# Scan pattern and reciprocals moved to SBUF, one forward scan for four pairs of heads, filler products alone in a PSUM bank, early low halves on VectorE

## The chip, the core and the metric

The kernel runs on one core of a Trainium2 chip. Its time is the device time of one execution in microseconds (us); the median of three runs is compared. The engines are TensorE (PE; its weight loads are listed as PEld), VectorE (DVE), ScalarE (ACT), GpSimd (POOL) and SyncE (SP), which issues most of the transfers. Each engine takes its instructions in the order in which the program lists them.

## The reference

A linear attention with a decay per channel feeds a mixture of experts with two choices a token, and that feeds a dense block (batch 4, 8 heads, 768 steps, head size 48; 3072 tokens of 384; 8 experts of 1024; dense width 2048).

```python
for t in range(S):                                   # attention
    state = alpha[:, :, t, :, None] * state + np.einsum('bhd,bhe->bhde', k[:, :, t], v[:, :, t])
    y[:, :, t] = np.einsum('bhd,bhde->bhe', q[:, :, t], state)
...
noisy_logits = x @ w_gate + np.log1p(np.exp(x @ w_noise)) * noise      # experts
top2 = np.argpartition(-noisy_logits, 2, axis=1)[:, :2]
...
    h = np.maximum(x[mask] @ w1[e], 0.0)
    out[mask] += top2_w[mask, k, None] * (h @ w2[e])
...
h = x @ w_in                                         # dense block
g = np.maximum(0.01 * h, h)
return (g @ w_out).astype(np.float32)
```

## The kernel before

The attention is cut into 24 units of 128 steps (`build_unit`), six for each batch row, in order. A unit holds four pairs of heads; its tables are 112 rows high, one pair side by side, so an operation over a unit is 112 x 512 (four pairs of 128 steps). `at` holds the decays, `kq` the keys and queries, `nv` the values; each is loaded once a unit by SyncE. For a unit VectorE does this:

- `back` (L965): a scan over all 512 columns from the right, `suf`, the product of the decays behind each step. Its second operand is a byte pattern that starts each pair anew.
- `forth` (L973, L974), twice, for two pairs each: the reciprocals of the pairs' totals are put into the first column of each pair of a float pattern, and a scan over 256 columns from the left with that pattern as its second operand gives `wt`.
- `keys` (L988) and `queries` (L992): `kt = k * suf` and `qp = q * wt`.

Both patterns lie in one PSUM tile, `pC`, of 512 columns: 256 for the float pattern of two pairs, 128 for the byte pattern, and the last 128 are where filler products are written (`warm`). Filler products (L919, `keep_busy`) are products of the identity with itself whose result nobody reads; they keep TensorE at work where the planner sees a pause.

From `kt` and `qp` TensorE makes the turned keys (`pM`, L1000), the scores (`pS`, L1013), the state's update (L1048, L1052), and the outputs within and across units (`pY`, L1069, L1076), and turns the output back with the router's logits beside it (`pA`, L1098). ScalarE copies the results out (`kN`, `ar`, `S`, `xt`, `xg`). GpSimd masks the scores (`am`, L1022, two a unit), multiplies the state by the decays' totals (`sp`, L1039) and makes the totals (`tots`, L978). After each four units (a tile) the router runs (`gate_top2` and what follows, all small operations `g_...`, `run`, `sel`, `pk`, `si`), and GpSimd scatters the four blocks of tokens to their experts' slots (L1191, two for each block).

The weights of an expert come in pieces of 384 KB; each is split into a high half by ScalarE (L464) and a low half, the rest, by `split_lo` (L468): `w1lA`, `w2lA` for expert 0 and `w1lB`, `w2lB` for half the pieces behind it. The low halves stand as "vg": VectorE or GpSimd, whichever the planner has free. The expert stage begins with the first product of L742 once the rows of the first group are turned (`xl`, L609) and the last tile's counts are through TensorE (L1162, L538).

The order of all engines is made by `Planner`, which plays the steps through with an estimated duration for each, a due time, and rings that say how many buffers of a tile there are. Where it sees TensorE pause for longer than `GAP`, it puts filler products in front of the next step, as many as the pause divided by `FILL` (or, for the first, by `COLD`).

Of the kernel before, what the change touches and what calls it, by code (L numbers as in the profile page):

```python
# [7 lines left out]
FT = mybir.dt.float32  # L8
# [3 lines left out]
U32 = mybir.dt.uint32  # L12
AF = mybir.ActivationFunctionType
OP = mybir.AluOpType
# [5 lines left out]
PERIOD = 6.0  # L20
# [13 lines left out]
TYD = 8.0  # L34
# [35 lines left out]
class Planner:  # L70

    NEAR, FAR, SLACK, RATE, LAND = 0.1, 0.25, 0.8, 0.26, 2.0
    GAP, FILL, COLD, AHEAD, MARGIN = 0.45, 0.24, 0.45, 0.3, 3.0

# [261 lines left out]
def tile_kernel(  # L336
# [21 lines left out]
    nc = tc.nc  # L358
# [5 lines left out]
    NG, C = 4, 128  # L364
    P2, HP, NC = 2 * D, H // 2, S // C

    PP = 64 + D
# [98 lines left out]
    def split_lo(i, which, en):  # L466
        hi, lo = WT[i][2 * which:2 * which + 2]
        (nc.vector if en == "v" else nc.gpsimd).tensor_sub(lo, RAW[i, which], hi.bitcast(FT))  # L468
# [180 lines left out]
    def build_experts(t0, R, scat, last_x, ready_at, totals, acc_done, begun):  # L649
# [33 lines left out]
        def expert_weights(i, after):  # L683
            e = PAIRS[i][1]
            prev = [WO[i - 1]] if i else []
            phase = 1 if e == 0 else 2
            AUX[i] = []
            for m, nm in enumerate(("w1s", "w2s")):
                fe = add("s", 0.45, lambda m=m: fetch(i, m), after, takes=[R[nm]], size=0.39)
                hi = add("a", 0.73, lambda m=m: split_hi(i, m), prev, use=[(fe, R[nm])] + ([(WO[i], R["W"])] if m else []),  # L690
                         takes=[] if m else [R["W"]], phase=phase)
                if m == 0:
                    WO[i] = hi
                AUX[i].append([hi, add("vg", dict(v=0.87, g=1.8), lambda en, m=m: split_lo(i, m, en), [hi],
                                       use=[(fe, R[nm]), (WO[i], R["W"])], phase=phase)])
# [208 lines left out]
    with ExitStack() as actx:  # L904
# [3 lines left out]
        psum = actx.enter_context(tc.tile_pool(name="psum", bufs=1, space=PSUM))  # L908
        bank = psum.tile([128, 512], FT, name="pC", bufs=1)
        scb, warm = bank[:PP, 0:HB * C + C], bank[:, HB * C + C:]  # L910
        nc.vector.memset(scb, 0.0)
        d1f = scb[:, 0:HB * C].rearrange("p (h c) -> p h c", c=C)
        d1b = scb[:, HB * C:].bitcast(mybir.dt.uint8)

        nc.vector.memset(scb[:, HB * C:].bitcast(U32).rearrange("p (h c) -> p h c", c=C // 4)[:, :, C // 4 - 1:], 1 << 24)

# [15 lines left out]
        def build_unit(u):  # L932
            d = st[u]
            b = at_unit(u)
            hc = HB * C
            prev = st[u - 1] if u else None
# [31 lines left out]

            def forth(i):
                if i == 0:  # L970
                    d["wt"] = work.tile([PP, NW], FT, name="wt", bufs=3)
                    d["wv"] = d["wt"].rearrange("p (h c) -> p h c", c=C)
                nc.vector.reciprocal(d1f[:, :, 0], d["sv"][:, i * HB:(i + 1) * HB, 0])  # L973
                nc.vector.tensor_tensor_scan(d["wt"][:, i * hc:(i + 1) * hc], d["at"][:, i * hc:(i + 1) * hc],  # L974
                                             scb[:, 0:hc], 0.0, OP.mult, OP.add)

# [5 lines left out]
            totals.append(tt)  # L982
            f0 = add("v", 0.8, lambda: forth(0), [b1], use=[(LA, R["at"]), (b0, R["suf"])], takes=[R["wt"]])
            f1 = add("v", 0.8, lambda: forth(1), [f0], use=[(LA, R["at"]), (b0, R["suf"]), (f0, R["wt"])])

# [124 lines left out]
            cy = add("a", 0.5, copy_y, [done], use=[(w0, R["pY"])], takes=[R["xt"]])  # L1110
            ty = add("p", 0.8, turn_y, [consts_in], use=[(cy, R["xt"])], takes=[R["pA"]], due=b + PERIOD + TYD)
            cx = add("a", 0.39, copy_x, use=[(ty, R["pA"])], takes=[R["xg"]])
# [369 lines left out]
```

## Time and profile before

| What | us |
|---|---|
| median of three runs | 1079.25 (1076.63 to 1081.55) |
| the profiled execution, its own time | 1087.71 |
| its span | 1085.9 |
| TensorE busy in the span | 1042.8 (96%) |
| VectorE busy | 593.7 (55%) |
| ScalarE busy | 388.2 (36%) |
| GpSimd busy | 278.5 (26%) |

The shares are means over two stages that have little in common: the attention with the router, up to 178.6 us, and the expert and dense products after it. Times in the rows are us from the span's start. A row of the timeline has a start, a duration, engine, line, operation, `out<-in`, shapes, and in brackets the idle time of the engine ahead of it and what ended it. TensorE does a product of 32-bit floats in two passes, so 11 products of the program are 22 rows of the trace.

### The profile page before, as it was taken

What the parts mean: (1) busy time and instruction counts of PE and PEld (TensorE: products, weight loads), DVE (VectorE), ACT (ScalarE), POOL (GpSimd) and SP (SyncE); (2) the same over time, 40 slices, a digit from 0 to 9 for tenths busy, and PEclk for the clock granted to TensorE, in tenths of its full rate; (3) what the DMA queues carried; (4) which work ended last, traced back from release to release, by engine and by line L of the source; (5) the groups of instructions that cost most, each with busy time, mean ns of one, the idle gap of its engine ahead of it and who ended that gap; (6) DMA issues with size and microseconds to landing.
All of it is one profiled execution on the core that took longest, in us unless ns stands there. A gap on an engine that the chain in (4) does not pass through costs nothing.

```text
span 1085.9 us, 18172 instructions
## 1 busy us (share of the span) xinstructions
PE 1042.8 (96%) x6839; PEld 999.2 (92%) x6839; DVE 593.7 (55%) x1218; ACT 388.2 (36%) x825; POOL 278.5 (26%) x321
## 2 busy tenths in 40 slices
PE   6999895999999999999999999999999999999997
PEld 5887775999999999999999989899999999999997
DVE  5998997223464565646574233455554545454543
ACT  3755644223354544445453222222222222212211
POOL 3466876200032253424351021410110100000000
PEclk9998997999999999999999999999999999999999
DMA  9667746413464565746567344320101100000000
GB/s 232 203 203 242 237 129 222 157 50 103 148 201 141 179 200 164 226 142 207 180 222 241 116 153 139 92 66 9 59 22 45 34 33 16 22 1 23 1 22 26
DMA packets 78917, 133.20 MB, mean 123 GB/s; under 512 B 8514, under 2 KB 56260, under 8 KB 78820
## 3 DMA queue, kind: packets, MB, share of 16 engines
q1 hardware_dynamic: 72292, 111.89, 33.2%
q0 software_dynamic: 6528, 20.06, 5.7%
q8 instruction: 56, 0.92, 0.4%
q14 instruction: 41, 0.34, 0.1%
HBM read 93.38 MB, written 38.54 MB: 121 GB/s over the span
## 4 chain that ended last, share of the span: by engine, by line
PE 87%; DVE 8%; issue 2%; DMA 1%; ACT 1%; another core or an unknown queue 1%; POOL 0%; DVEq 0%; ACTq 0%; POOLq 0%
PE py L781 39%; PE ph L742 39%; PE pA L600 2%; DVE wt L974 1%; PE pS L1013 1%; DVE suf L965 1%; PE pA L1098 1%; PE pY L1069 1%; PE pC L919 1%; PE pY L1076 1%; DVE kt L988 1%; PE pM L1048 1%; DMA xg<-y_d,gidx 1%; DVE g_z L225 0%
## 5 line engine op out<-in xcount | busy, mean ns | idle before, releaser
L766 DVE SCALAR_TENSOR_TENSOR hl<-ph,hh 128x384 fp32r<-128x384 f32 (+1 forms) x128 | 77.4, 606 | 192.3 <-ACT hh L759 186.1
L752 ACT ACTIVATE hc<-ph 128x384 f32<-128x384 f32 x128 | 63.0, 492 | 300.6 <-PE ph L742 283.3
L755 DVE SCALAR_TENSOR_TENSOR hc<-hc 128x384 f32<-128x384 f32 x128 | 71.4, 558 | 178.2 <-ACT hc L752 178.2
L759 ACT ACTIVATE hh<-ph 128x384 fp32r<-128x384 f32 (+1 forms) x128 | 68.0, 532 | 241.7 <-PE ph L742 236.0
L781 PE MATMUL py<-w2hA,hh 128*128 128x384 f32 (+1 forms) x416 | 141.5, 340 | 1.1 <-issue 1.1
L781 PE MATMUL py<-w2hB,hh 128*128 128x384 f32 (+1 forms) x416 | 141.9, 341 | 0.2 <-issue 0.2
L781 PE MATMUL py<-w2lB,hh 128*128 128x384 f32 (+1 forms) x416 | 140.5, 338 | 0.4 <-issue 0.4
L781 PE MATMUL py<-w2hB,hl 128*128 128x384 f32 (+1 forms) x416 | 140.5, 338 | 0.0
L781 PE MATMUL py<-w2hA,hl 128*128 128x384 f32 (+1 forms) x416 | 140.0, 337 | 0.0
L781 PE MATMUL py<-w2lA,hh 128*128 128x384 f32 (+1 forms) x416 | 139.9, 336 | 0.0
L742 PE MATMUL ph<-xh,w1hA 128*128 128x384 f32 (+1 forms) x384 | 136.4, 355 | 1.4 <-ACT hc L752 0.7
L742 PE MATMUL ph<-xl,w1hA 128*128 128x384 f32 (+1 forms) x384 | 134.3, 350 | 1.0 <-issue 1.0
L742 PE MATMUL ph<-xh,w1hB 128*128 128x384 f32 (+1 forms) x384 | 134.1, 349 | 0.4 <-DVE hl L766 0.4
L742 PE MATMUL ph<-xh,w1lA 128*128 128x384 f32 (+1 forms) x384 | 134.1, 349 | 0.0
L742 PE MATMUL ph<-xl,w1hB 128*128 128x384 f32 (+1 forms) x384 | 133.4, 347 | 0.0
L742 PE MATMUL ph<-xh,w1lB 128*128 128x384 f32 (+1 forms) x384 | 133.3, 347 | 0.0
L804 POOL DMA_INDIRECT xg<-y_d,gidx x48 | 46.5, 968 | 279.6 <-PE pA L600 172.7
L781 PEld LDWEIGHTS py<-w2lA,hh 128*128 128x128 f32 (+1 forms) x416 | 77.3, 186 | 2.2 <-issue 1.2
L781 PEld LDWEIGHTS py<-w2lB,hh 128*128 128x128 f32 (+1 forms) x416 | 77.6, 187 | 1.3 <-issue 0.3
L781 PEld LDWEIGHTS py<-w2hB,hh 128*128 128x128 f32 (+1 forms) x416 | 77.5, 186 | 0.8
L769 DVE TENSOR_TENSOR hl<-hc,hh 128x384 fp32r<-128x384 f32 x128 | 71.4, 558 | 12.3 <-DVE hh L761 0.5
L781 PEld LDWEIGHTS py<-w2hB,hl 128*128 128x128 f32 (+1 forms) x416 | 77.6, 187 | 0.5 <-issue 0.5
(160 smaller groups left out, 1877.3 us busy)
## 6 DMA issues: line engine op xcount, KB each, us to landing
w1s<-in_moe_w_dram SPq DMA_DIRECT2D x32, 384.0 KB
w2s<-in_moe_w_dram SPq DMA_DIRECT2D x32, 384.0 KB
kq<-in_kq_l_dram SPq DMA_DIRECT2D x24, 448.0 KB
nv<-in_v_l_dram SPq DMA_DIRECT2D x24, 256.0 KB
w1s<-in_moe_w_in_dram SPq DMA_DIRECT2D x24, 256.0 KB
w2s<-in_moe_w_out_dram SPq DMA_DIRECT2D x16, 384.0 KB
xg<-x_s SPq DMA_DIRECT2D x32, 180.0 KB
y_d<-ys SPq DMA_DIRECT2D x32, 180.0 KB
```

The costliest lines, as they stand in the source:

```text
L600: nc.tensor.transpose(p[:, d, :n], src[:n, d * 128:(d + 1) * 128], identf[:n, :n])
L742: nc.tensor.matmul(ps[:, :n], a[:, d, fo:fo + 128], x[:, d, :n], start=i == 0, stop=i == len(seq) - 1)
L752: nc.scalar.activation(hc[:, :n], ps[:, :n], AF.Copy)
L755: nc.vector.scalar_tensor_tensor(hc[:, :n], hc[:, :n], 0.01, hc[:, :n], op0=OP.mult, op1=OP.max)
L759: nc.scalar.activation(hh[:, :n], ps[:, :n], AF.Relu)
L766: nc.vector.scalar_tensor_tensor(hl[:, :n], ps[:, :n], 0.0, hh[:, :n].bitcast(FT), op0=OP.max, op1=OP.subtract)
L769: nc.vector.tensor_sub(hl[:, :n], HT[si, "hc"][:, :n], hh[:, :n].bitcast(FT))
L781: nc.tensor.matmul(py[:n, :], h[:, o:o + n], w[:, f % 2, :], start=(f == 0 and i == 0), stop=(f == nf - 1 and i == 2))
L804: nc.gpsimd.indirect_dma_start(out=yg, out_offset=None, in_=y_d[0:rows, :], in_offset=bass.IndirectOffsetOnAxis(ap=gidx[:, c, kk:kk + 1], ...
L919: nc.tensor.matmul(warm, identf, identf, start=True, stop=True)
L965: nc.vector.tensor_tensor_scan(rev(d["suf"][:, :]), rev(d["at"][:, 1:NW + 1]), rev(d1b), 0.0, OP.mult, OP.add)
L974: nc.vector.tensor_tensor_scan(d["wt"][:, i * hc:(i + 1) * hc], d["at"][:, i * hc:(i + 1) * hc], scb[:, 0:hc], 0.0, OP.mult, OP.add)
```

## The change

The byte pattern and the float pattern become tiles of their own in SBUF, the float pattern now for four pairs; `forth` is one reciprocal of four columns and one scan of 512. The filler products keep `pC` for themselves, a tile of 128 columns. The low halves of expert 0 may go on VectorE alone. Four numbers of the planner change: two prices of a filler product, the price of the turn (`ty`), and the forward scan's.

```diff
-    GAP, FILL, COLD, AHEAD, MARGIN = 0.45, 0.24, 0.45, 0.3, 3.0
+    GAP, FILL, COLD, AHEAD, MARGIN = 0.45, 0.16, 0.22, 0.3, 3.0
...
-                AUX[i].append([hi, add("vg", dict(v=0.87, g=1.8), lambda en, m=m: split_lo(i, m, en), [hi],
+                AUX[i].append([hi, add("vg" if phase == 2 else "v", dict(v=0.87, g=1.8) if phase == 2 else 0.87, lambda en="v", m=m: split_lo(i, m, en), [hi],
...
-        bank = psum.tile([128, 512], FT, name="pC", bufs=1)
-        scb, warm = bank[:PP, 0:HB * C + C], bank[:, HB * C + C:]
-        nc.vector.memset(scb, 0.0)
-        d1f = scb[:, 0:HB * C].rearrange("p (h c) -> p h c", c=C)
-        d1b = scb[:, HB * C:].bitcast(mybir.dt.uint8)
-
-        nc.vector.memset(scb[:, HB * C:].bitcast(U32).rearrange("p (h c) -> p h c", c=C // 4)[:, :, C // 4 - 1:], 1 << 24)
+        warm = psum.tile([128, 128], FT, name="pC", bufs=1)
+        d1f = ac.tile([PP, HP, C], FT, name="d1f")
+        d1w = ac.tile([PP, HP, C // 4], U32, name="d1b")
+        nc.vector.memset(d1w, 0)
+        nc.vector.memset(d1w[:, :, C // 4 - 1:], 1 << 24)
+        nc.vector.memset(d1f, 0.0)
+        d1b = d1w.rearrange("p h c -> p (h c)").bitcast(mybir.dt.uint8)
...
-            def forth(i):
-                if i == 0:
-                    d["wt"] = work.tile([PP, NW], FT, name="wt", bufs=3)
-                    d["wv"] = d["wt"].rearrange("p (h c) -> p h c", c=C)
-                nc.vector.reciprocal(d1f[:, :, 0], d["sv"][:, i * HB:(i + 1) * HB, 0])
-                nc.vector.tensor_tensor_scan(d["wt"][:, i * hc:(i + 1) * hc], d["at"][:, i * hc:(i + 1) * hc],
-                                             scb[:, 0:hc], 0.0, OP.mult, OP.add)
+            def forth():
+                d["wt"] = work.tile([PP, NW], FT, name="wt", bufs=3)
+                d["wv"] = d["wt"].rearrange("p (h c) -> p h c", c=C)
+                nc.vector.reciprocal(d1f[:, :, 0], d["sv"][:, :, 0])
+                nc.vector.tensor_tensor_scan(d["wt"][:, :], d["at"][:, 0:NW], d1f.rearrange("p h c -> p (h c)"), 0.0,
+                                             OP.mult, OP.add)
...
-            f0 = add("v", 0.8, lambda: forth(0), [b1], use=[(LA, R["at"]), (b0, R["suf"])], takes=[R["wt"]])
-            f1 = add("v", 0.8, lambda: forth(1), [f0], use=[(LA, R["at"]), (b0, R["suf"]), (f0, R["wt"])])
+            f0 = f1 = add("v", 1.35, forth, [b1], use=[(LA, R["at"]), (b0, R["suf"])], takes=[R["wt"]])
...
-            ty = add("p", 0.8, turn_y, [consts_in], use=[(cy, R["xt"])], takes=[R["pA"]], due=b + PERIOD + TYD)
+            ty = add("p", 0.98, turn_y, [consts_in], use=[(cy, R["xt"])], takes=[R["pA"]], due=b + PERIOD + TYD)
```

The order of instructions follows from the planner. First VectorE at the program's start, before, with what each row waits for (a semaphore of an engine, or of a transfer's queue, DMAHW); `pC` is the shared tile.

```order
L965 SCALAR_TENSOR_TENSOR suf<-at,pC 112x512 [waits DMAHW0_49,DVE_49]
L973 RECIPROCAL pC<-suf 112x2 [waits DVE_49]
L974 SCALAR_TENSOR_TENSOR wt<-at,pC 112x256 [waits DVE_49]
L988 TENSOR_TENSOR kt<-kq,suf 112x512 [waits DMAHW1_49]
L973 RECIPROCAL pC<-suf 112x2 [waits DVE_49]
L974 SCALAR_TENSOR_TENSOR wt<-at,pC 112x256 [waits DVE_49]
L965 SCALAR_TENSOR_TENSOR suf<-at,pC 112x512 [waits DMAHW2_49,PE_49]
L992 TENSOR_TENSOR qp<-kq,wt 112x512 [waits DVE_49]
```

The same place in the changed program, where `d1b` and `d1f` are the patterns in SBUF:

```order
L964 SCALAR_TENSOR_TENSOR suf<-at,d1b 112x512 [waits DMAHW0_49,DVE_49]
L971 RECIPROCAL d1f<-suf 112x4 [waits DVE_49]
L972 SCALAR_TENSOR_TENSOR wt<-at,d1f 112x512 [waits DVE_49]
L985 TENSOR_TENSOR kt<-kq,suf 112x512 [waits DMAHW1_49]
L989 TENSOR_TENSOR qp<-kq,wt 112x512 [waits DVE_49]
L964 SCALAR_TENSOR_TENSOR suf<-at,d1b 112x512 [waits DMAHW2_49]
```

One reciprocal and one forward scan stand where two of each stood, `qp` moved ahead of the next unit's backward scan, and that scan's wait for TensorE (PE) is gone.

Next TensorE at the program's start, before:

```order
L919 MATMUL pC<-identf 128x128 x11
L1000 MATMUL pM<-identf,kt 128x112 x4
L919 MATMUL pC<-identf 128x128 x8
L1013 MATMUL pS<-qp,kt 128x128 x8
L1048 MATMUL pM<-nv,kN 64x48
```

And in the changed program:

```order
L919 MATMUL pC<-identf 128x128 x26
L997 MATMUL pM<-identf,kt 128x112 x4
L1010 MATMUL pS<-qp,kt 128x128 x8
L919 MATMUL pC<-identf 128x128 x7
L1045 MATMUL pM<-nv,kN 64x48
```

The first filler row grew from 11 products to 26, and the second moved behind the first scores and is one shorter.

Last GpSimd at the end of the attention, before (L468 is a low half, L1191 a scatter; rows between the two pieces are left out):

```order
L468 TENSOR_TENSOR w1lA<-w1s,w1hA 128x768
L1022 AFFINE_SELECT am<-ar 128x512 x2
L1039 TENSOR_TENSOR sp<-S,tots 112x192
L978 TENSOR_TENSOR tots<-suf,at 112x4
L468 TENSOR_TENSOR w2lA<-w2s,w2hA 128x768
...
L1191 DMA x_s<-xg,si 6913x384 x7
L468 TENSOR_TENSOR w1lB<-w1s,w1hB 128x768
L468 TENSOR_TENSOR w2lB<-w2s,w2hB 128x768
L1191 DMA x_s<-xg,si 6913x384 x10
```

And in the changed program, where no `w1lA` or `w2lA` is left on GpSimd in the attention:

```order
L1188 DMA x_s<-xg,si 6913x384
L1036 TENSOR_TENSOR sp<-S,tots 112x192
L1188 DMA x_s<-xg,si 6913x384
L1019 AFFINE_SELECT am<-ar 128x512 x2
L1036 TENSOR_TENSOR sp<-S,tots 112x192
L1188 DMA x_s<-xg,si 6913x384 x8
L468 TENSOR_TENSOR w1lB<-w1s,w1hB 128x768
L468 TENSOR_TENSOR w2lB<-w2s,w2hB 128x768
L468 TENSOR_TENSOR w1lB<-w1s,w1hB 128x768
L1188 DMA x_s<-xg,si 6913x384 x8
```

Five low halves of expert 0 left GpSimd (three `w1lA`, two `w2lA`); all eight stand on VectorE behind the last unit's `qp`. Between the fifth and the sixth tile's scatters GpSimd has three low halves where it had two.

## Rows read from the trace of the kernel before

**Rows 1.** Stretches: their bounds, length, then busy us (instructions) of each engine.

```profile
core 0: us, PE busy (x) PEld busy (x) DVE busy (x) ACT busy (x) POOL busy (x), PEclk, DMA share, GB/s
...
29.60:150.80 121.20, 113.07 (x1450) 95.91 (x1448) 112.05 (x277) 74.55 (x179) 78.40 (x107) 0.94 0.68 209
...
178.60:1086.00 907.40, 894.89 (x5036) 873.00 (x5035) 442.15 (x848) 290.87 (x595) 169.37 (x160) 0.99 0.33 105
```

**Rows 2.** Waits of VectorE, 3 to 180 us: total, times, longest.

```profile
DVE suf L965 <- PE pC L919: 5.0, 1, 5.0
DVE pC L973 <- PE pC L919: 4.5, 3, 3.0
```

**Rows 3.** Timeline of the start, units 0 and 1.

```profile
5.01 0.17 DVE L973 RECIPROCAL pC<-suf 112x2 f32<-112x2 f32 x1
...
5.22 0.69 DVE L974 TENSOR_TENSOR_SCAN wt<-at,pC 112x256 f32<-112x256 f32 x1
...
5.83 0.67 DVE L988 TENSOR_TENSOR kt<-kq,suf 112x512 f32<-112x512 f32 x1
...
7.44 4.80 PE L919 MATMUL pC<-identf 128*128 128x128 f32 x22 [7.44 <-DVE wt L974]
...
7.93 0.64 ACT L959 ACTIVATE scr<-at 112x517 bf16<-112x517 f32 x1 [3.52 <-DMA at<-in_al_l_dram]
...
12.28 1.22 DVE L965 TENSOR_TENSOR_SCAN suf<-at,pC 112x512 f32<-112x512 f32 x1 [4.98 <-PE pC L919]
...
13.41 0.67 DVE L992 TENSOR_TENSOR qp<-kq,wt 112x512 f32<-112x512 f32 x1
```

**Rows 4.** Groups of VectorE, 29.6 to 150.8: busy us, mean ns, idle before.

```profile
L974 DVE TENSOR_TENSOR_SCAN wt<-at,pC 112x256 f32<-112x256 f32 x40 | 27.4, 686 | 1.4
L965 DVE TENSOR_TENSOR_SCAN suf<-at,pC 112x512 f32<-112x512 f32 x20 | 24.0, 1207 | 0.0
L988 DVE TENSOR_TENSOR kt<-kq,suf 112x512 f32<-112x512 f32 x20 | 14.9, 745 | 0.0
...
L973 DVE RECIPROCAL pC<-suf 112x2 f32<-112x2 f32 x40 | 6.7, 168 | 1.1 <-PE pC L919 0.9
...
L292 DVE TENSOR_TENSOR wts<-g_wd,g_ws 128x4 f32<-128x4 f32 x3 | 0.5, 182 | 0.0
```

**Rows 5.** Groups of GpSimd in the same stretch.

```profile
L1022 POOL TENSOR_SCALAR_AFFINE_SELECT am<-ar 128x512 f32<-128x512 f32 x39 | 27.3, 710 | 10.1 <-ACT ar L1017 10.0
L1039 POOL TENSOR_TENSOR sp<-S,tots 112x192 f32<-112x192 f32 x16 | 9.4, 585 | 4.7 <-ACT S L1057 3.8 <-ACT g_ln L209 0.8
L468 POOL TENSOR_TENSOR w1lA<-w1s,w1hA 128x768 fp32r<-128x768 f32 x3 | 5.4, 1813 | 0.0
```

**Rows 6.** One stretch of the start, and the transfers' sizes.

```profile
15.00:18.00 3.00, 3.00 (x15) 3.00 (x16) 0.47 (x1) 0.00 (x0) 0.00 (x0) 0.54 1.05 250
...
kq<-in_kq_l_dram SPq DMA_DIRECT2D x24, 448.0 KB
nv<-in_v_l_dram SPq DMA_DIRECT2D x24, 256.0 KB
at<-in_al_l_dram SPq DMA_DIRECT2D x24, 226.2 KB
```

**Rows 7.** Timeline, router of the fourth tile.

```profile
136.73 1.82 POOL L468 TENSOR_TENSOR w1lA<-w1s,w1hA 128x768 fp32r<-128x768 f32 x1
136.89 1.74 DVE L1149 TENSOR_TENSOR_SCAN run<-msk,ot 128x32 bf16<-128x32 bf16 x1
```

**Rows 8.** Timeline, router of the last tile.

```profile
173.56 0.19 DVE L229 TENSOR_TENSOR g_z<-g_z,noise_sb 128x32 f32<-128x32 f32 x1
...
177.06 0.22 DVE L1149 TENSOR_TENSOR_SCAN run<-msk,ot 128x32 bf16<-128x32 bf16 x1
```

**Rows 9.** Timeline of the tail.

```profile
166.71 0.23 DVE L1107 TENSOR_REDUCE lg<-pA 128x16 f32<-128x64 f32 x1 [3.18 <-issue]
...
169.27 4.25 DVE L225 TENSOR_TENSOR g_z<-g_ln,g_um 128x32 f32<-128x32 f32 x1
...
178.37 0.94 DVE L468 TENSOR_TENSOR w1lB<-w1s,w1hB 128x768 fp32r<-128x768 f32 x1
```

More of the change, by code (lines that the diff above doesn't have):

```diff
@@ L934, in build_unit @@
             b = at_unit(u)
-            hc = HB * C
             prev = st[u - 1] if u else None
```

## The prediction

> **What bounds the kernel now.** I read the table of stretches first [rows 1]. From 178.6 us on TensorE is busy for 894.89 of 907.40 us: the expert stage is a block of products that begins when the first of them may begin, and the diff changes none of its work. So the question is when that block begins. Ahead of it lie the attention units: 121.20 us in which VectorE is busy for 112.05 and TensorE for 113.07, so neither has much to spare, and a tail of 27.8 us. I count to three points on VectorE: the backward scan of unit 4 (29.6), the last `qp` (150.8), the first expert product (178.6).
>
> Next I asked what VectorE waits for [rows 2]. Two lines name the filler products: 5.0 us once and 4.5 us in three waits, of which 0.9 lies in the middle stretch [rows 4]. The timeline shows the first [rows 3]: `pC` filler 7.44 to 12.24, and the backward scan of unit 1 starting at 12.28 after 4.98 us of waiting, though its input was there at 7.93, when ScalarE took the same tile. Before, pattern and filler share one tile.
>
> Last the costs of VectorE and GpSimd over the middle stretch [rows 4, 5].
>
> **The change, part by part.** The profiled run took 1087.71 us, 1.8 more than its span, and the median shown is 1079.25; differences are worked out against the profiled run and put on the median.
>
> *Filler alone in its bank.* The new order has no wait for TensorE at the scans, so these waits go: 5.0 + 4.5 - 0.9 = 8.6 us before 29.6, and 0.9 later. Can loads follow? Units 0 to 3 need four `at`, four `kq` and, by the order of issue, two `nv`: 4 x 226 + 4 x 448 + 2 x 256 KB = 3.2 MB; at the 250 GB/s of [rows 6] that is 13 us behind the first load, about 15 us, while `kq` of unit 3 would be wanted at about 18. So the loads hide. The first filler row grows from 11 products to 26, 52 passes. They wait for the identity alone. The 22 old passes took 4.80 us [rows 3]; 52 at that pace would take 11.3 us from about 1.4, to 12.7, half a microsecond behind the old row's end, and VectorE no longer waits for it. Gain at the start: 8.6 us; bounds 4 (TensorE, about as late as before, holds `kt` back) and 8.6.
>
> *One forward scan, one reciprocal.* From start to start a reciprocal takes 0.21 and a half scan 0.61 (5.01, 5.22, 5.83 in [rows 3]); twice that is 1.64. A whole scan takes 1.13 (12.28 to 13.41, the backward one). So 1.64 - 0.21 - 1.13 = 0.30 us a unit: 1.2 us in the first four, 6.0 in the other twenty. That a forward scan of 512 costs as much as a backward one is taken; at twice the half scan the gain would be 0.21, 1.8 us less in all.
>
> *Both scans now read two SBUF operands.* This is the dear part. Of such scans the trace has one kind, the short `run`: 0.22 us when GpSimd is elsewhere [rows 8], 1.74 us when GpSimd was in a subtraction that lasted until 138.55 [rows 7]; it ended at 138.63. Beside it the half scans of `wt`, which read their pattern from PSUM, take 686 ns in all 40 rows' mean, `suf` 1207, whatever GpSimd does [rows 4]. So a scan with two SBUF inputs waits for GpSimd's reader to end, one with a PSUM pattern does not.
>
> How much? In the middle stretch the seventeen two-input kinds, from `kt` to the last `wts`, are 121 instructions and 59.2 us; all 277 rows add to 128.3 us and cover 112.05, so 0.06 of each overlaps its neighbour, and these hold 52 us, a share of 0.43. Undisturbed, `kt` and `qp` take 0.67 (41 of them) and the small ones 0.19 [rows 3, 8]: 59.2 - 27.5 - 15.2 = 16.5 us are waits. GpSimd's readers in the stretch, at their undisturbed 0.64, 0.52 and 1.81: 39 `am` 25 us, 16 `sp` 8.3, five low halves 9.1, together 42.4 [rows 5]. VectorE thus paid 0.39 of GpSimd's time, 0.91 of its own share. After: the low halves leave (33.3 us stay), and the share rises: 52 - 16.5 + 40 scans of 1.13 = 80.7 us and the waits W, in 121.2 - 16.5 - 6.0 - 0.9 + W = 97.8 + W. W = 33.3 x 0.91 x (80.7 + W)/(97.8 + W) gives 26 us, 9.5 more than now. Middle stretch: 97.8 + 26 - 121.2 = **+2.6**. Bounds: every scan waits only as `kt` does (0.745 - 0.67 = 0.08, 3.2 us for 40) and the share of the low halves goes (0.39 of 9.1, 3.5 us): W = 16, -7.2; VectorE pays all 33.3: +9.9. I take 26 because the scans start, as the small ones do, right after work of their own unit frees GpSimd. In the first stretch, by the same rate, six `am` and two `sp` (4.9 us) cost 0.91 x 0.86 x 4.9 = 3.8, against 1.1 for `kt` and `qp` there now: 2.7 more.
>
> The Trainium skill, page "SBUF — State Buffer", section "Who interferes with whom", has it as a rule: an instruction of VectorE with at most one SBUF input stays clear of GpSimd, one with two contends with a GpSimd instruction that reads SBUF, and whoever comes second stands still for the whole of the other. The `run` row agrees. Taken as a lock that is always met it is the upper bound, and the rival "slower" below.
>
> *Low halves on VectorE.* The five that GpSimd did in the middle stretch now stand behind the last `qp` on VectorE: 5 x 0.94 = 4.7 us in the tail. There it was idle 3.18 us for the last logits and some 0.7 more [rows 9], so about 1 us shows. GpSimd has three second-pair low halves behind the scatters of the fifth tile, where two stood; beside them `g_z` took 4.25 us instead of 0.19, on the path to the first product. A third adds up to 1.81. Together +2.8 (0 to 6.5).
>
> *GpSimd's side.* It waits for scans as they wait for it; its busy 78.40 of 121.20 us [rows 1] leaves room, less 9.1 us of low halves. But each `am` stands ahead of products in TensorE's order. In some four places of the middle such a wait reaches the path; half a scan each is +2.4 (0 to 8).
>
> *Planner numbers.* 0.98 for the turn and the filler's prices only reorder; cover is the slack above, their price lies inside these bounds.
>
> Sum: -8.6 - 1.2 + 2.7 = -7.1 at the start, +2.6, +2.8, +2.4: **+0.7 us**. The start has more on the losing side (its bound is 4, not 8.6), so I put 1.3 on it: +2, **1081 us**.
>
> **Rivals.** Half a per cent, 5.4 us, is about what a measurement here tells from no change.
>
> Faster: the scans wait no more than `kt` does. Then -9.8 at the start, -7.2 in the middle, which the 8.1 us that TensorE has to spare there just allow, +1 in the tail: -16, 1063. For it: `kt` and `qp`, the large two-input operations, lose only 0.08 each now. Against: they run right behind a PSUM scan in which GpSimd has finished its work; that cover is gone.
>
> Slower: VectorE and GpSimd alternate on the shared reader. W is 33.3, GpSimd's scatters slip behind the scans, and TensorE, in order, waits for `am`: start -5, middle +9.9, tail +4, GpSimd +8: +17, 1096. It decides from W of 30 on. For it: 80.7 + 33 us of the stretch would be readers of SBUF, nearly all of it. Against: 36 of GpSimd's 78.40 busy us are other work, nearly all of it scatters.
>
> Nothing happens at the start: TensorE, which runs its long filler first, holds the units to their old pace; -1 instead of -7.1: +6.8, 1086. It counts with slower.
>
> **Chances.** Gains and waits cancel (within 5.4 us): 0.41. Slower, by either way: 0.38. Faster: 0.21. The likeliest has 1075 to 1085 as its own range; 8 in 10 reach from 1067 to 1097.
>
> **What would show it.** Unit 1's backward scan at about 8 us, not 12.28, and no wait of VectorE for `pC`. `wt` 24 times at 1.2 undisturbed, with a mean over 1.3, and a mean of `suf` above 1.21, its longest rows ending where an `am` or `sp` ends. The last `qp` near 146, the first expert product near 179. I am wrong if scans keep one length beside GpSimd, if unit 4 starts no sooner than 26, or if TensorE's idle time in the middle grows by more than 5 us.

## The result and the profile after

The changed kernel takes 1085.62 us (median of 20 runs, 1082.47 to 1093.17), the kernel before 1080.6 beside it: a ratio of 1.0059, 95% interval 1.0045 to 1.0072. A second set of runs, on another chip, gives 1.0069 (1.0040 to 1.0098). It is slower by six or seven tenths of a per cent. The time lies inside the range on record, 1067 to 1097, just above the 1075 to 1085 that "gains and waits cancel" had as its own. By the number it answers to the third rival, "nothing happens at the start", for which 1086 was worked out.

The chips differ (the kernel before took 1080.3 to 1091.6 us in the sets below), so kernels are compared by their ratio to the kernel before in the same set, and profiles by a pair taken on one chip. First before, then after: the table by stages, cut at the backward scan of unit 8, behind the last `qp`, and at the first expert product. Columns: stretch, its length, busy time (and instructions) of each engine, granted clock, DMA share, GB/s.

```profile
core 0: us, PE busy (x) PEld busy (x) DVE busy (x) ACT busy (x) POOL busy (x), PEclk, DMA share, GB/s
0.00:52.00 52.00, 42.44 (x514) 37.56 (x516) 38.20 (x83) 27.36 (x65) 17.27 (x49) 0.97 0.80 218
52.00:155.90 103.90, 91.62 (x1130) 76.63 (x1128) 92.79 (x225) 58.61 (x140) 70.59 (x94) 0.93 0.65 202
155.90:183.50 27.60, 15.29 (x168) 12.35 (x164) 20.56 (x66) 11.36 (x26) 18.53 (x19) 0.81 0.65 213
183.50:1089.00 905.50, 893.35 (x5036) 872.63 (x5035) 439.71 (x848) 290.51 (x595) 169.29 (x160) 0.99 0.34 105
```

```profile
0.00:55.40 55.40, 48.59 (x531) 42.43 (x533) 39.73 (x68) 27.54 (x65) 18.76 (x49) 0.85 0.74 199
55.40:157.90 102.50, 93.13 (x1076) 79.36 (x1074) 92.86 (x192) 53.69 (x131) 77.38 (x85) 0.85 0.59 187
157.90:188.10 30.20, 17.37 (x212) 14.34 (x208) 26.77 (x69) 16.29 (x36) 24.08 (x24) 0.85 0.81 256
188.10:1100.00 911.90, 897.75 (x5033) 873.82 (x5032) 439.97 (x850) 289.73 (x594) 170.00 (x161) 0.99 0.33 105
```

The start is 3.4 us longer where 7.1 were to be saved, the middle 1.4 shorter, the tail 2.6 longer, and the expert stage, which the diff leaves alone, 6.4 longer. TensorE's granted clock moved most: 0.97 to 0.85 at the start, 0.93 to 0.85 in the middle. Both profiles of after are of executions slower than its median (1093.17 us, the slowest of 20, and 1102.53 where the median is 1100.45), so this pair differs by 11.4 us where the ratio makes it 7.5.

The timeline of the first profile of after shows the start. Columns: start, duration, engine, line, operation, tiles, and in brackets the idle time ahead of it and what ended it.

```profile
3.84 1.23 DVE L964 TENSOR_TENSOR_SCAN suf<-at,d1b 112x512 f32<-112x512 f32 x1 [2.09 <-DMA at<-in_al_l_dram]
7.64 1.22 DVE L964 TENSOR_TENSOR_SCAN suf<-at,d1b 112x512 f32<-112x512 f32 x1
...
16.92 1.03 POOL L1228 COPY turn_w<-wgn 128x64 f32<-128x64 f32 x1 [11.57 <-DMA wgn<-in_wgp_l_dram]
18.51 1.23 POOL L1019 TENSOR_SCALAR_AFFINE_SELECT am<-ar 128x512 f32<-128x512 f32 x2
...
19.21 2.55 PE L1066 MATMUL pY<-am,nv 128*64 128x128 f32 x16 [5.71 <-POOL am L1019]
...
21.12 1.23 DVE L964 TENSOR_TENSOR_SCAN suf<-at,d1b 112x512 f32<-112x512 f32 x1 [0.84 <-DMA at<-in_al_l_dram]
...
37.58 0.22 DVE L1104 TENSOR_REDUCE lg<-pA 128x16 f32<-128x64 f32 x1 [10.63 <-PE pA L1095]
```

VectorE did what was forecast: the backward scan of unit 1 starts at 7.64 instead of 12.28 [rows 3], that of unit 4 at 21.12 instead of 29.58. Then it stands for 10.63 us at the first logits, and unit 8 begins later than before (55.41, before 51.66). The logits wait for TensorE, TensorE for the first `am`, and that `am` stands on GpSimd behind a copy of `wgn`, a small table for the router's logits. Its load is issued behind the ten loads of the first units, at 7.48, and lands at 16.9. At the end of its 5.71 us of idling TensorE's granted clock falls to half (1.2 of 2.4 GHz) and stays there for 13.65 us:

```profile
18.51:32.16 13.65, 12.95 (x102) 10.70 (x102) 7.53 (x7) 4.86 (x11) 6.62 (x12) 0.50 0.72 186
```

The scans, over the attention stage of the same profile (duration min/median/max in ns, first and last start), and one of them on the timeline:

```profile
L972 DVE TENSOR_TENSOR_SCAN wt<-at,d1f x24: 1224/1225/2879, 5.3 to 152.9; 112x512 f32<-112x512 f32 x24
L964 DVE TENSOR_TENSOR_SCAN suf<-at,d1b x24: 1192/1218/1689, 3.8 to 151.4; 112x512 f32<-112x512 f32 x24
```

```profile
84.22 2.41 DVE L972 TENSOR_TENSOR_SCAN wt<-at,d1f 112x512 f32<-112x512 f32 x1
84.34 1.22 POOL L1019 TENSOR_SCALAR_AFFINE_SELECT am<-ar 128x512 f32<-128x512 f32 x2
```

Undisturbed, a forward scan takes 1.22 us. This one took 2.41: it ended 1.07 us after both `am` were through, at 85.56, as if it had waited for them before it ran. The mean of the 24 `wt` is 1.47 us, that of `suf` 1.25.

The tail, on VectorE and GpSimd:

```profile
180.81 0.19 DVE L254 TENSOR_REDUCE g_cm<-g_ca 128x4 f32<-128x32 f32 x1
181.03 4.24 DVE L258 TENSOR_TENSOR g_oh<-g_ca,g_cm 128x32 f32<-128x32 f32 x1
181.64 1.82 POOL L468 TENSOR_TENSOR w1lB<-w1s,w1hB 128x768 fp32r<-128x768 f32 x1
183.41 1.81 POOL L468 TENSOR_TENSOR w2lB<-w2s,w2hB 128x768 fp32r<-128x768 f32 x1
185.31 0.19 DVE L265 SCALAR_TENSOR_TENSOR g_z<-g_oh,g_z 128x32 f32<-128x32 f32 x1
```

As before [rows 9], one small router operation lasts until the two low halves that GpSimd does beside it are through. That is not always so. In the profile of before in the tables above, the same two low halves held two operations, one each:

```profile
174.89 1.81 POOL L468 TENSOR_TENSOR w1lB<-w1s,w1hB 128x768 fp32r<-128x768 f32 x1 [1.19 <-issue]
174.91 1.84 DVE L221 TENSOR_TENSOR g_um<-g_um,g_ru 128x32 f32<-128x32 f32 x1
...
176.66 1.80 POOL L468 TENSOR_TENSOR w2lB<-w2s,w2hB 128x768 fp32r<-128x768 f32 x1
...
176.78 1.73 DVE L225 TENSOR_TENSOR g_z<-g_ln,g_um 128x32 f32<-128x32 f32 x1
```

### The profile page after: what moved, and what is told of

It reads as the page before. It is cut to its first block, busy times and chain, and to the rows that moved or that the text cites. A ratio compares the mean times of both kernels' runs of the same rounds, so it can differ in the third digit from the quotient of the medians.

```text
span 1091.5 us, 18135 instructions
## 1 busy us (share of the span) xinstructions
PE 1051.0 (96%) x6841; PEld 1007.5 (92%) x6841; DVE 602.2 (55%) x1175; ACT 387.9 (36%) x825; POOL 288.5 (26%) x317
## 4 chain that ended last, share of the span: by engine, by line
PE 85%; DVE 6%; issue 4%; POOL 2%; DMA 2%; ACT 1%; DVEq 0%; POOLq 0%; ACTq 0%; SPq 0%
PE py L781 39%; PE ph L742 39%; PE pA L600 2%; PE pY L1066 1%; PE pS L1010 1%; PE pY L1073 1%; DVE suf L964 1%; POOL x_s L1188 1%; DVE wt L972 1%; PE pA L1095 1%; DMA at<-in_al_l_dram 1%; DVE g_oh L258 1%; DMA xg<-y_d,gidx 1%; DVE kt L985 0%; DVE qp L989 0%
## 5 line engine op out<-in xcount | busy, mean ns | idle before, releaser
L781 PEld LDWEIGHTS py<-w2hA,hh 128*128 128x128 f32 (+1 forms) x416 | 77.3, 186 | 0.8
```

Of the source, the lines that this page charges most:

```text
L781: nc.tensor.matmul(py[:n, :], h[:, o:o + n], w[:, f % 2, :], start=(f == 0 and i == 0), stop=(f == nf - 1 and i == 2))
```

## The experiments

**The load of `wgn` first.**

```diff
-        ld = add("s", 0.14, load_consts, lat=2.5, due=at_unit(1))
+        ld = add("s", 0.14, load_consts, lat=2.5, due=-100.0)
```

> The changed kernel with one number altered: the load of the router's small constants (wgn) is the first in SyncE's queue instead of standing behind the units' first loads. My theory: the start's gain is lost because GpSimd, in order, stands 11.57 us behind the copy of wgn until 16.92, so the first am comes at 18.51, TensorE idles 5.71 us, its granted clock is 0.5 from 18.51 to 32.16, and VectorE then waits 10.63 us at 37.58 for the first logits. Then the first am comes near 9 to 11, the half clock there is gone or shorter, the scan of unit 8 starts 4 to 8 us before 55.41, and the time is 5 to 7 us less than the changed kernel's, near 1079. Rival (the numbers of the planner, or TensorE's long filler, hold the units): the first am is early but unit 8 starts within 2 us of 55.41, and the time stays within 2 us of the changed kernel's, near 1085.

Ratio 1.0012 (0.9991 to 1.0032): 0.47% or 5 us less than the changed kernel. The timeline, and the stretch in which the clock had been halved:

```profile
6.10 0.24 POOL L1228 COPY turn_w<-wgn 128x64 f32<-128x64 f32 x1
...
11.95 2.45 POOL L1019 TENSOR_SCALAR_AFFINE_SELECT am<-ar 128x512 f32<-128x512 f32 x2 [1.94 <-ACT ar L1014]
...
27.73 0.21 DVE L1104 TENSOR_REDUCE lg<-pA 128x16 f32<-128x64 f32 x1
```

```profile
18.51:32.16 13.65, 13.18 (x177) 11.23 (x174) 13.51 (x19) 8.41 (x20) 10.97 (x11) 1.00 1.05 264
```

The first `am` comes at 11.95 instead of 18.51, TensorE does 177 passes instead of 102 in the same 13.65 us (a product is two passes), at full clock, the first logits come ten microseconds sooner, and unit 8 starts at 45.32, 10.1 us earlier than in the changed kernel and 6.3 earlier than before. The start's loss was the load, and the rival falls. Half of the ten microseconds is given back later.

**The filler apart, pattern kept in PSUM** (on the kernel before, same order on every engine; the ten later filler products are left out).

```diff
-        scb, warm = bank[:PP, 0:HB * C + C], bank[:, HB * C + C:]
+        scb, early = bank[:PP, 0:HB * C + C], [psum.tile([128, 512], FT, name="pY", bufs=1)[:, 0:128]]
...
-            for _ in range(n):
-                nc.tensor.matmul(warm, identf, identf, start=True, stop=True)
+            for _ in range(n if early else 0):
+                nc.tensor.matmul(early[0], identf, identf, start=True, stop=True)
...
             def within():
+                early.clear()
```

> The kernel before, every engine's instructions in the same order, but its filler products go to the bank of the first output product, so that scans share no tile with them; the ten filler products later on are left out (nobody reads them). Scan patterns stay in PSUM. This is the first part of the change without its contention. My theory (the start is held by GpSimd, which stands behind wgn): unit 1's backward scan at about 8 us instead of 12.28, but the first am still at 18 or later, unit 8 no sooner than 49 (51.66 before), and the time within 2 us of before. Rival (the prediction's step: 8.6 us of waits go): unit 4 starts near 21 instead of 29.58, unit 8 near 43 to 45, and the time is 5 to 9 us less.

Ratio 0.9978 (0.9957 to 0.9999): 2.4 us, not 8.6. Its timeline:

```profile
7.20 1.19 DVE L965 TENSOR_TENSOR_SCAN suf<-at,pC 112x512 f32<-112x512 f32 x1
...
16.68 0.24 POOL L1231 COPY turn_w<-wgn 128x64 f32<-128x64 f32 x1 [11.43 <-DMA wgn<-in_wgp_l_dram]
17.02 1.24 POOL L1022 TENSOR_SCALAR_AFFINE_SELECT am<-ar 128x512 f32<-128x512 f32 x2
...
17.72 2.56 PE L1069 MATMUL pY<-am,nv 128*64 128x128 f32 x16 [4.33 <-POOL am L1022]
...
27.12 0.22 DVE L1107 TENSOR_REDUCE lg<-pA 128x16 f32<-128x64 f32 x1 [7.52 <-ACT xg L1102]
```

The wait of VectorE for the filler is gone (7.20), and 7.52 us of waiting stand at the first logits in its place; unit 8 starts at 51.58 (51.66 before). The filler's wait had been hiding the wait for `wgn`. The first `am` came at 17.02, not at 18 or later. Behind TensorE's 4.33 us of idling its clock is at half from 16.56 to 26.80; in the kernel before, where filler products run in that time, it was so only from 15.27 to 18.68. How much of the 7.52 us is the load and how much the clock, this run does not part.

**Patterns in SBUF, nothing else** (the kernel before; still two half scans).

```diff
-        bank = psum.tile([128, 512], FT, name="pC", bufs=1)
-        scb, warm = bank[:PP, 0:HB * C + C], bank[:, HB * C + C:]
+        warm = psum.tile([128, 128], FT, name="pC", bufs=1)
+        scb = ac.tile([PP, HB * C + C], FT, name="scb")
```

> The kernel before with only the tiles changed: the scan pattern in SBUF, the filler alone in its PSUM tile; two half scans, low halves and numbers stay as before. My theory: the waits for the filler at the start go (up to 8.6 us off the start of unit 4's scan, though not all of it reaches unit 8), and all scans now read two SBUF operands, so the mean of suf rises above 1.21 and of the half scans above 0.69, some 3 to 10 us in the middle; the time is within 4 us of before. Rival (scans are not touched by GpSimd): suf and wt keep 1.21 and 0.69 and the time is 4 to 8 us less than before. If the start's loss lies in GpSimd's wait for wgn, the first am is at 18 or later here too, and unit 8 starts no sooner than 51.

Ratio 1.0115 (1.0088 to 1.0142), 12 us more, three times the bound that I had given it. Beside the run above, which has the filler apart and the pattern in PSUM, the place of the pattern costs 1.4%, some 15 us (the two sets ran on different chips, and the run above also lacks the later filler products). The first `am` came at 16.81 and unit 8 at 50.75, both sooner than I had named. The groups and the timeline:

```profile
L974 DVE TENSOR_TENSOR_SCAN wt<-at,scb x48: 690/692/3519, 5.1 to 160.0; 112x256 f32<-112x256 f32 x48
```

```profile
150.43 1.81 POOL L468 TENSOR_TENSOR w2lA<-w2s,w2hA 128x768 fp32r<-128x768 f32 x1
150.44 2.35 DVE L974 TENSOR_TENSOR_SCAN wt<-at,scb 112x256 f32<-112x256 f32 x1
```

A half scan of 0.69 us takes 2.35 behind a low half of GpSimd; over all 48 the mean goes from 0.69 to 0.97, and the stretch from unit 8 to the last `qp` from 98.5 and 103.3 us in the two profiles of before to 111.3.

**Only the forward scan's pattern back in PSUM** (the changed kernel, same order; filler as in the filler run).

```diff
-        warm = psum.tile([128, 128], FT, name="pC", bufs=1)
-        d1f = ac.tile([PP, HP, C], FT, name="d1f")
+        early = [psum.tile([128, 512], FT, name="pY", bufs=1)[:, 0:128]]
+        d1f = psum.tile([128, HP, C], FT, name="pC", bufs=1)[:PP]
```

> The changed kernel, every engine's instructions in the same order, but the forward scan's pattern is a PSUM tile of a whole bank again, so that this scan reads one SBUF operand; the filler products before unit 0's first output product go to that product's own bank, and the three filler products later on are left out (nobody reads them). The backward scan still reads two SBUF operands. My theory (a scan with two SBUF operands waits for GpSimd's readers): wt goes from a mean of 1470 ns to 1224 to 1240 in all 24, which is 24 x 0.24 = 5.9 us of VectorE, and the time is 3 to 6 us less than the changed kernel's, 1080 to 1083. Rival (VectorE waits just as long somewhere else, in kt or in the small two-input operations, or for TensorE): wt gets short, but the time stays within 2 us of the changed kernel's 1085.6.

Ratio 0.9998 (0.9972 to 1.0024), 0.6% less than the changed kernel, which was measured on other chips; the place of the filler changed with it. From its profile only durations are read:

```profile
L972 DVE TENSOR_TENSOR_SCAN wt<-at,pC x24: 1220/1221/1222, 5.2 to 147.4; 112x512 f32<-112x512 f32 x24
L964 DVE TENSOR_TENSOR_SCAN suf<-at,d1b x24: 1192/1216/1551, 3.7 to 146.0; 112x512 f32<-112x512 f32 x24
```

From 1224 to 2879 ns with the pattern in SBUF, to 1220 to 1222 in all 24 with it in PSUM, beside the same GpSimd work: in these rows a scan waits when both of its operands lie in SBUF, and only then. The Trainium skill, page "SBUF — State Buffer", section "Who interferes with whom", has this rule, and these rows agree with it. The backward scan, which still reads two, goes on waiting a little.

**Both edits together.**

> The two edits together: forward scan's pattern in PSUM (filler in the output product's bank) and the load of wgn first in SyncE's queue. If start and contention are separate losses the gains add: 4.5 (measured for wgn) and 3 to 6, so 1075 to 1078, 3 to 5 us less than the kernel before. Rival (both gains end at the same later wait): 1080 to 1081, no better than the better one alone.

Ratio 0.9968 (0.9941 to 0.9995): 3.5 us less than before, where adding the two gains would give 5; the interval holds both. Its last `qp` is at 137.81 and the first expert product at 168.98, 12.3 and 9.6 us ahead of the first profile of before, but TensorE then idles 3.6 us between 186 and 191, of which 2.57 for `hl` of VectorE, which itself waits for ScalarE's `hh`. By this profile part of what attention gains is lost at the expert stage's first products.

**The low halves shared again** (the changed kernel).

```diff
-                AUX[i].append([hi, add("vg" if phase == 2 else "v", dict(v=0.87, g=1.8) if phase == 2 else 0.87, lambda en="v", m=m: split_lo(i, m, en), [hi],
+                AUX[i].append([hi, add("vg", dict(v=0.87, g=1.8), lambda en, m=m: split_lo(i, m, en), [hi],
```

> The changed kernel with the early weights' low halves again free to go to GpSimd, as before. Theory: low halves on VectorE behind the last qp lengthen the tail (from the last qp to the first expert product 33.8 us against 28.45 before); then the tail falls by 3 to 5 us, the middle stretch grows by 1 to 3 us because GpSimd's 1.8 us reads come back beside the scans, and the time is 1 to 4 us less than the changed kernel's. Rival (the tail is long because of the half clock there and the router's own operations): the tail stays within 1.5 us of 33.8 and the time is the same or up to 3 us more.

Ratio 1.0113 (1.0090 to 1.0137): 5.8 us more than the changed kernel, and the theory falls; so does the rival, which had the tail unchanged and at most 3 us more. The tail does shorten, from 33.8 to 23.6 us, but the stall moves behind the first expert products:

```profile
180.30 3.87 DVE L221 TENSOR_TENSOR g_um<-g_um,g_ru 128x32 f32<-128x32 f32 x1
...
184.66 4.27 DVE L233 TENSOR_TENSOR g_z<-g_z,lg 128x32 f32<-128x32 f32 x1
...
192.66 0.69 PE L742 MATMUL ph<-xh,w1hA 128*128 128x384 f32 x1 [8.65 <-DVE hl L766]
```

Two router operations are held, `hl` stands behind them on VectorE, and TensorE waits 8.65 us for it. Over the attention stage the mean `kt` is 0.99 us instead of 0.76 and that of `suf` 1.34 instead of 1.25, while `wt` (1.46) and `qp` (0.71) take no longer than in the changed kernel.

**The low halves alone on VectorE** (the kernel before, with the reverse of that diff).

> The kernel before with the last part of the change alone: the early weights' low halves on VectorE only. By the prediction's rate each of the five low halves that GpSimd did in the middle stretch cost VectorE 0.39 x 1.81 = 0.7 us, together 3.5, and the five on VectorE are worth 4.7 us behind the last qp, of which most is hidden in waits there: 0 to 3 us less than before. Rival (the second run, in which sharing them again cost the changed kernel 6.6 us, carries over): 4 to 7 us less. Other rival (the low halves lengthen the tail): 2 to 5 us more.

Ratio 0.9977 (0.9962 to 0.9993), 2.5 us less than before, by the prediction's rate for such waits. This part of the change is a gain. In the changed kernel, where the scans can wait too, the run above makes it 5.8; the intervals of the two numbers still overlap.

**The second pair's low halves on VectorE as well** (the changed kernel).

```diff
-add("vg" if phase == 2 else "v", dict(v=0.87, g=1.8) if phase == 2 else 0.87, lambda en="v", m=m
+add("vg" if e > 1 else "v", dict(v=0.87, g=1.8) if e > 1 else 0.87, lambda en="v", m=m
```

> The changed kernel with the low halves of the second pair of weights on VectorE too, so that GpSimd reads no SBUF beside the router's last operations. Theory: the 4.24 us that one g_ operation takes beside two such low halves (0.2 undisturbed) stands on the path to the first expert product; then no g_ operation takes over 1 us there, the tail from the last qp falls by 2 to 4 us from 33.8, and the time by 1 to 3 us. Rival (the expert stage makes up for a late start anyway, since its first products wait for weights): the tail falls, the time stays within 1 us of the changed kernel's.

No operation of the last tile's router takes over 0.25 us any more; the tail is 30.5 us (30.7 in the changed kernel beside it), the ratio 1.0063 (1.0043 to 1.0083), against 1.0069 there. The held operation in the tail shows no cost by itself. The rival was right on the time, though the tail that it saw falling did not fall, and the two intervals are too wide to rule out the theory's 1 to 3 us.

**The planner's numbers of before.**

```diff
-    GAP, FILL, COLD, AHEAD, MARGIN = 0.45, 0.16, 0.22, 0.3, 3.0
+    GAP, FILL, COLD, AHEAD, MARGIN = 0.45, 0.24, 0.45, 0.3, 3.0
...
-            ty = add("p", 0.98, turn_y, [consts_in], use=[(cy, R["xt"])], takes=[R["pA"]], due=b + PERIOD + TYD)
+            ty = add("p", 0.8, turn_y, [consts_in], use=[(cy, R["xt"])], takes=[R["pA"]], due=b + PERIOD + TYD)
```

> The changed kernel with the planner's three numbers of before (filler 0.24 and 0.45, turn 0.8). My theory puts nothing on them: within 2 us of the changed kernel's time. Rival: the cheaper filler price, which makes the first filler row 26 products instead of 11 or so, pushes the first units' products back and is where the start's gain goes; then the time is 4 to 6 us less, near 1080, and the scan of unit 8 starts near 51 instead of 55.41.

Ratio 1.0067 (1.0042 to 1.0092): no difference, and unit 8 starts at 55.33. The long filler at the start is not the cause.

**Before and after again, on one chip.**

> The kernel before, unchanged, for a profile on the same chip as the three kernels beside it. In the two profiles compared so far the expert stage (first expert product to the end) is 907.35 us before and 901.58 after, TensorE idle in it 5.67 and 1.90 us, which the change does not explain. If that difference belongs to the chip and not to the kernel, the two profiles taken here have expert stages within 2.5 us of each other once waits that hang on the tail (the first 25 us) are taken out; if it belongs to the change, before is again about 4 to 6 us longer, with stalls near 686 us that after lacks.

> The changed kernel, unchanged, on the same chip as its neighbours: a second measurement of the ratio, 1.004 to 1.008 by the first (1.0045 to 1.0072). By my theory its first am is again at 18 or later, TensorE's granted clock falls to half behind it, and unit 8 starts 2 to 5 us later than before's. If the start's loss was an accident of the one profile, unit 8 starts with before's or ahead of it.

These are the tables by stages above, and the second ratio. The first `am` of after is at 18.29, its clock half from 15.37 to 32.44, and unit 8 at 55.40 against 51.96. But the size of this loss is not fixed. Two kernels above, the one with shared low halves and the one with the second pair's low halves on VectorE, have the changed kernel's instructions in its order on all four compute engines up to unit 8. Their half clock and their unit 8, the latter kernel first (it ran on the chip of this pair):

```profile
17.22:20.63 3.41, 3.37 (x24) 2.74 (x26) 3.41 (x4) 0.78 (x2) 2.56 (x3) 0.50 0.86 245
```

```profile
50.20 2.33 DVE L964 TENSOR_TENSOR_SCAN suf<-at,d1b 112x512 f32<-112x512 f32 x2
```

```profile
17.72:27.96 10.24, 10.09 (x83) 8.79 (x84) 8.61 (x9) 4.44 (x10) 6.54 (x9) 0.50 1.00 240
```

```profile
52.49 2.33 DVE L964 TENSOR_TENSOR_SCAN suf<-at,d1b 112x512 f32<-112x512 f32 x2
```

Their first `am` comes at 16.55 and 16.64, TensorE idles 2.75 and 2.60 us for it, and unit 8 starts 1.8 us ahead of before in the one and 2.9 ahead of after in the other. With the load late in all four, unit 8 comes the later the longer the clock stays at half: 50.20 behind 3.41 us, 52.49 behind 10.24, 55.4 behind 13.65 and 17.07. So the two profiles of after show the dear end of what the late load costs.

The forecast for the expert stage was half right. The stalls near 690 go with the chip, not with the kernel: 12 us of TensorE of before and of after on this chip, and of the first profile of after:

```profile
688.00:700.00 12.00, 9.16 (x46) 8.84 (x45) 6.79 (x14) 3.98 (x8) 5.79 (x7) 0.86 0.38 105
```

```profile
700.00:712.00 12.00, 9.25 (x46) 7.61 (x45) 5.19 (x11) 3.87 (x8) 5.28 (x6) 1.00 0.36 102
```

```profile
691.00:703.00 12.00, 12.00 (x70) 12.00 (x69) 8.07 (x17) 3.98 (x8) 9.26 (x10) 1.00 0.52 149
```

The first two lose 2.8 us each and the third none; the profile shows nothing that these waits were for. The first profile of before has such waits too (2.5 us between 686 and 692, and its clock at half from 691.10 to 694.51). So the first pair of profiles made the change look some four microseconds cheaper in this stage than it is. The longer expert stage of after in the pair above (6.4 us) lies within its first 28: TensorE idles 3.7 us between 204 and 212, most of it again for nothing that the profile shows, and its clock is at half from 209.93 to 216.76.

**The parts that gained, without those that cost.** On the kernel before: filler in the first output product's bank, `wgn` first, low halves on VectorE; patterns in PSUM, two half scans (the three diffs above).

> The parts that gained, on the kernel before: patterns of both scans stay in PSUM (two half scans as before), the filler products go to the first output product's bank, the load of wgn is first in SyncE's queue, the early weights' low halves are on VectorE only; the later filler products are left out (nobody reads them). If the measured parts add (0.2% for the filler, 0.2% for the low halves, 0.4 to 0.5% for wgn), the ratio to before is 0.991 to 0.993, below the 0.997 of the version with one forward scan. Rival (with the attention stage shorter, the expert weights' loads and the router's tail are what comes last, as in that version, where 12 us at the last qp left 3.5 at the end): 0.996 to 0.998.

Ratio 0.9889 (0.9864 to 0.9915): 1079.8 us where the kernel before took 1091.55, 12 us less. The parts by themselves (0.22, 0.23, and 0.47% for `wgn`, that one measured in the changed kernel) add to 0.991, inside the interval. Its table by stages:

```profile
0.00:44.20 44.20, 40.80 (x512) 35.79 (x514) 38.55 (x82) 27.53 (x65) 18.20 (x49) 1.00 0.99 245
44.20:140.10 95.90, 87.25 (x1130) 74.71 (x1127) 86.15 (x224) 55.61 (x136) 62.20 (x86) 0.95 0.65 199
140.10:172.00 31.90, 18.11 (x153) 14.53 (x152) 26.09 (x73) 13.31 (x29) 22.35 (x22) 0.70 0.74 245
172.00:1079.00 907.00, 895.54 (x5034) 873.67 (x5032) 440.22 (x847) 292.11 (x597) 169.93 (x160) 0.99 0.34 105
```

The start is 7.8 us shorter than that of before on the same chip, with the clock at 1.00 throughout, the middle 8.0 shorter, the tail 4.3 longer, the expert stage 1.5 longer. The forward scans are twice as many as in the changed kernel and all undisturbed.

## Why the prediction was right or wrong

The number fell into the range; the account behind it failed at one step and held, in kind, at two. That the number lay inside is owed more to the width of the range, 30 us, than to the account, since the start alone came out 10.9 us off in the first pair.

- **Start: forecast -7.1, counted at unit 4; measured there -8.5 and -9.0 in the two pairs, but +3.8 and +3.4 at unit 8.** The gain was counted at a point behind which it is lost again: from unit 4 to the last `qp`, where +2.6 was forecast, the changed kernel takes 14.4 and 11.1 us more. The step that failed is "So the loads hide". I counted `at`, `kq` and `nv` of the first units, and not the load behind them on which another engine waits: GpSimd takes its instructions in order, and its copy of `wgn` stands ahead of the first `am`. VectorE's next wait, for logits that need that `am`, lies behind unit 5. The kernel before has the wait for `wgn` too; there VectorE was held by the filler meanwhile. That ending the filler's wait gives little by itself is shown by the filler run (2.4 us), that the load is the cause by the first run (5 us); with the filler apart and the load first, in the last run, the start is 7.8 us shorter, about what had been forecast. The rival "nothing happens at the start" named the wrong engine: TensorE did not hold the units with its filler, whose 52 passes ended at 9.13 and not at 12.7; it was starved, and then ran at half clock.
- **The contention of the scans: right in kind.** The middle as it is from unit 8 on, behind the wait for the logits, took +2.2 and -1.4. The waits W can be read on the forecast's own stretch, from unit 4 to the last `qp`, as the time of VectorE's instructions with two SBUF inputs over the shortest of their kind: 17.0 and 19.8 us before, 24.7 and 22.6 after, where the step has 16.5 and 26. So the step "VectorE pays 0.91 of its share" was somewhat too dear for a kernel in which the low halves have left GpSimd. What the forward scan's pattern costs in the end is about 0.6% there, and about 1.4% for both scans while the low halves are still on GpSimd; both numbers compare sets of different chips, and the filler differs with the pattern.
- **Low halves: forecast +2.8 in the tail, against 3.5 us off the middle by the rate of 0.39; measured as one part, a gain.** By themselves they give 2.5 us, in the changed kernel 5.8. I priced them in the tail, where the held router operation was visible. The tail's length is no price: what is saved there shows up as a wait at the first expert products, as the two runs on low halves show.
- **One forward scan: forecast -7.2 in all (-1.2 and -6.0).** Not measured apart. The kernel with patterns in SBUF and two half scans, and the changed kernel with shared low halves, which has one scan and the new numbers, have the same ratio (1.0115 and 1.0113); 7.2 us would be 0.0067, more than their intervals leave room for. A whole forward scan takes 1.14 us from start to start (5.31 to 6.45), as was taken; at twice the half scan the loss would have been 2.2 us over all units, and not 1.8. Either the part gives little, since VectorE's time was not what TensorE waited for, or something in the new order takes it back; that stays open.
- **GpSimd's backlog: forecast +2.4.** Not measured apart. The nearest numbers are of TensorE between unit 8 and the last `qp`: it idles 8.1 us before and 11.1 after in the first pair, 12.4 and 9.4 in the second, at a granted clock of 0.93 before and 0.90 and 0.85 after.
- **Planner numbers at nothing: right** (1.0067 against 1.0059 and 1.0069).

Of the signs that were to show it, unit 1's scan at 8, no wait for `pC`, `wt` with a mean over 1.3 (1.47), and `suf` above 1.21 (1.25 and 1.22) came as written. The last `qp` (156.07) and the first expert product (189.87) came ten microseconds late, and for "unit 4 no sooner than 26" I had watched a point that was too early. TensorE's idle time in the middle, from unit 4 on, grew by 3.0 us in the first pair and fell by 3.1 in the second, so that sign of being wrong did not come. The longest `suf` (70.24 to 71.92) does not end where an `am` or `sp` ends, as I had said it would.

## What to carry to other kernels

Before a wait is counted as a gain, look for the next thing that the waiting engine needs, and follow it back over every engine's queue to a load: a small table that sits late in a load queue can hold a whole pipeline through an engine that takes its work in order, and a longer wait elsewhere hides it. A tile that an operation of VectorE reads many times is worth a place in PSUM when GpSimd reads SBUF beside it, and the dearest neighbours are GpSimd's long subtractions. Price an edit at the end of the stage that waits for it, with runs of the part alone and of the whole without it, since neither the point where it acts nor one pair of profiles gave the sum here.

## What the runs showed of the hardware

- An operation of VectorE with two SBUF operands can wait out several GpSimd instructions in a row: 4.24 us for two low halves of 1.8, and 2.41 for a scan of 1.22 behind two `am`. It need not: 1.84 and 1.73 us for two operations beside the same two low halves in the second profile of before. In the long case the operation had started 0.61 us ahead of the first low half; why it waited for both is not shown.
- The times of one kernel's runs go with TensorE's granted clock: the 20 runs of after go from 1082.47 us at a mean of 0.983 to 1093.17 at 0.971. A wait of TensorE at the start is followed by a stretch at half clock, whose length is not in the length of the wait alone: 5.71 us (13.5 to 19.2) by 13.65 in the first profile of after and 5.37 by 17.07 in the second; 2.75 by 3.41 and 2.60 by 10.24 in two kernels with the same instructions up to there; 2.31 us up to a filler product at 14.94 by 3.41 in the first profile of before.
- On some chips TensorE loses 1.9 to 2.8 us between 676 and 714, most of it for nothing that the profile shows: all eight profiles of two sets of runs have it, whatever the kernel, and all four of another set have not.
